# Two of three patterns of VectorE's exponentials added by DMA in a two-branch attention kernel

## The chip, the cores and the metric

The kernel runs on one core of one Trainium2 chip. The metric is the device time of one execution in microseconds (us), the median of several runs; lower is better.

## What is computed

Two independent attention blocks on inputs of 2048 rows and 512 columns, 32 heads of 16 columns each; the two results stand side by side in the output. Branch A is linear attention, branch B is softmax attention:

```
# A
phi = lambda t: jnp.where(t > 0, t + 1, jnp.exp(t)) + 1e-6
kv = jnp.einsum("bhsd,bhse->bhde", pk, v)
num = jnp.einsum("bhqd,bhde->bhqe", pq, kv)
o = num / den
...
# B
scores = jnp.einsum("bhqd,bhkd->bhqk", q, k) * scale
p = _softmax(scores, axis=-1)
o = jnp.einsum("bhqk,bhkd->bhqd", p, v)
```

Each branch has its own projections (x times wqkv) ahead of this and an output projection (times wo) behind it. Most of the work is B: 32 heads times 2048 x 2048 scores, each through an exponential.

## The kernel before

**Tiling.** Branch B is cut into 32 units. A unit is four heads (one per group of 32 rows of TensorE) and 512 queries. It holds 64 blocks: four heads times sixteen tiles of 128 keys. A block is a 128 x 512 piece of transposed scores. For each block one score matmul (line 946) fills a bank of PSUM with 128 keys by 512 queries; an engine takes the exponential into SBUF; value matmuls (line 1355) multiply it with the values and add into one bank per unit. The values have 16 columns and a column of ones, which gives the sum of the exponentials. Matmuls of four heads run beside one another on TensorE, score matmuls in four row groups and value matmuls in four column groups.

**Two ways to an exponential.** ScalarE (line 1161) reads two or three adjacent banks and writes the exact exponential as 16-bit floats into the buffer PT of 25 blocks; each of its blocks needs one value matmul. VectorE (line 1065) scales and offsets a block's scores and writes them as 16-bit integers whose bits, read as 16-bit floats, approximate the exponential. To make the approximation better, three such patterns are summed: the base pattern, weighted by 1.55 (VW, held in a scaled copy VX of the values), and two patterns that are the same integers plus 328 and plus 656 (SHIFT). The additions are made by GpSimd (line 1245) on the integers, four at a time as one 64-bit word; two blocks form a group, and one addition makes one pattern of a group. So a VectorE block needs three value matmuls: one with VX for the base pattern, two with VV for the shifted patterns. The buffer DI holds eight groups of three patterns (planes) of 2 x 512 values each.

**Order.** All instructions of all engines are written out at build time by a planner. It keeps a clock for each engine (T), a cost for each operation, candidates for each engine, and picks step by step what starts next; what it picks is appended to that engine's list. Each engine runs its list in order, and semaphores are derived from what is read and written. The choices around the change:

- `d_pick` (line 1004) decides whether a block goes to VectorE: a bank must be free, VectorE's and GpSimd's backlogs must be under limits (DBL, PBL), and a DI buffer must be free.
- `fill_act_cand` (line 1094) fills score banks for ScalarE, and puts blocks for VectorE beside them.
- `chain` (line 1199) follows when a group is complete; its inner `on_pool` (line 1221) emits the two additions, and `plain` (line 1214) would make them on VectorE late in the last unit.
- `pv_cand` (line 1282) batches value matmuls whose inputs are planned to be ready, up to a few rounds of four.
- Jobs for the projections, branch A and the outputs are filled in between. Their transfers are issued by SyncE, and a job that depends on one becomes available after a planned time: 6.5 us for the spread of the keys (line 678), 7.0 us for a transposed piece of A's input (line 482), 2.6 us for a transpose of A's output (line 859).
- The table SEG (line 274) holds 28 settings of the planner for each 12 us of planned time: limits, priorities, round sizes, and a seed for small random choices.

The costs that the planner uses are constants, among them:

```
PFX = 0.173
PEL = 0.00041
...
d = 0.0635 + w * 0.000833
...
waiting[bi] = (buf, b, push("dve", en + LTO["pe", "dve"], 0, 0.598, p1))
```

An addition is planned at PFX plus PEL for each of its 16-bit elements, an exponential on ScalarE at d for w columns, one on VectorE at 0.598 us, a round of value matmuls at 0.2185 us.

Of the kernel before, what the change touches and what calls it, by code (L numbers as in the profile page):

```python
# [10 lines left out]
F16 = mybir.dt.float16  # L11
# [228 lines left out]
def bass_concat_heads__linear_attn_block__softmax_full_mha__prompt_kernel(nc, A_x, A_wqkv, A_wo, B_x, B_wqkv, B_wo, out):  # L240
# [8 lines left out]
    LAY = (25, 8)  # L249
    PW = 0.5  # L250
# [6 lines left out]
    NDG = LAY[1]  # L257
# [9 lines left out]
    DE3 = 0  # L267
# [87 lines left out]
    XAL = 7.0  # L355
# [10 lines left out]
    TRACE = None  # L366
    PEB = 14
# [7 lines left out]
    with es:  # L375
# [19 lines left out]
        DIR = 3 * DGW  # L395
        DI = sb("DI", [128, NDG * DIR], I16)

        def di_at(v, b):

            return b * DIR + v * DGW  # L400
# [166 lines left out]
        port = {"pool": 0.0, "dve": (0.0, 0.0)}  # L567

# [84 lines left out]
        def proj_job(Gp, sc, kind, fast=False, **kw):  # L653
# [24 lines left out]
            def spread(bk):  # L678
                for e_ in range(2):
# [4 lines left out]
            st.append(("dma", 6.5, spread))  # L684
# [75 lines left out]
        def chunked(st, i):  # L760

            eng, dur, fn = st[3]
            def done(bk):
                fn(bk)
                xa_left[i] -= 1
                if xa_left[i] == 0 and i + 2 < 12:
                    load_xa(i + 2)
                    tok[("xA", i + 2)] = T["pe"] + XAL
            st[3] = (eng, dur, done)
            return st  # L770
# [27 lines left out]
        def akvsum_job(hp, bl, **kw):  # L798
# [7 lines left out]
            if hp == bl == 1:  # L806
                st.append(("dma", 14.0, lambda bk: load_wo()))
# [24 lines left out]
        def anum_job(sc, tl, **kw):  # L832
            pq = sc % 2
            o2 = tl % 2
            def f(e, bk):
                for bq in range(4):
# [6 lines left out]
                            RD[:, pq, tl * 32:tl * 32 + 32].unsqueeze(2).broadcast_to([128, 32, 16]), op=ALU.mult), [("RD", pq)], oak(o2))), ("dma", 2.6, lambda bk: ont_load(o2))],  # L843
# [15 lines left out]
        def ont_load(o2):  # L859
# [943 lines left out]
```

## Time and profile before

| what | value |
|---|---|
| median of 3 runs (range) | 644.63 us (644.21 to 644.69) |
| the profiled execution | 644.23 us |
| its span, first to last instruction | 642.5 us |
| mean granted TensorE clock | 0.998 |
| DMA packets, bytes | 53230, 21.80 MB |

The profile is one execution. Its page lists, for each engine, the time that it was busy and its share of the span; then groups of instructions by line of the kernel, with the count, the busy time, the mean duration of one in ns, and the idle time of that engine just before them with what ended it. A duration includes a tail in which the next instruction already runs, so the time that an instruction costs is read from the distance between starts in the timeline. In the stretches, each engine has its busy time and its count in parentheses; the last three columns are the granted clock, the mean busy share of the 16 DMA engines, and GB/s.

### The profile page before, as it was taken

How to read it: one execution, taken by the hardware profiler on the slowest of the kernel's cores; microseconds unless marked ns; L12 is line 12 of the kernel's file. 1: busy time of each engine (PE TensorE's matmuls, PEld its weight loads, DVE VectorE, ACT ScalarE, POOL GpSimd, SP SyncE). 2: the span in 40 equal slices, each digit the busy share in tenths (PEclk: the TensorE clock that was granted, in tenths of full speed). 3: DMA queues.
4: the chain of work that ended last, by engine and by line, in shares of the span. 5: the costliest groups of instructions: out<-in, count | busy, mean ns of one | idle time of the engine just before them, and what ended most of it. 6: DMA issues, size and time to landing. Idle time of an engine off the chain costs nothing.

```text
span 642.5 us, 20026 instructions
## 1 busy us (share of the span) xinstructions
PE 635.4 (99%) x8562; PEld 218.1 (34%) x8562; DVE 612.0 (95%) x1086; ACT 628.7 (98%) x692; POOL 440.5 (69%) x751
## 2 busy tenths in 40 slices
PE   8999999999999999999999999999999999999997
PEld 6333332333333333343333333223222322223243
DVE  6999999999999999999999999999999999999985
ACT  6999999999999999999999999999999999999995
POOL 4666788876767766657767676677776668766751
PEclk9999999999999999999999999999999999999999
DMA  9701000002010011012021012002110110000112
GB/s 187 209 2 24 21 1 12 8 3 43 3 35 1 2 35 35 10 35 45 18 50 51 3 41 45 17 10 50 28 34 10 27 34 18 26 11 26 35 43 71
DMA packets 53230, 21.80 MB, mean 34 GB/s; under 512 B 44176, under 2 KB 52624, under 8 KB 53136
## 3 DMA queue, kind: packets, MB, share of 16 engines
q1 hardware_dynamic: 51664, 19.80, 13.3%
q8 instruction: 69, 1.13, 0.7%
q10 hardware_dynamic: 1472, 0.66, 0.4%
q14 instruction: 25, 0.20, 0.1%
HBM read 4.46 MB, written 4.19 MB: 13 GB/s over the span
## 4 chain that ended last, share of the span: by engine, by line
PE 68%; ACT 31%; DVE 1%; issue 0%
ACT PT L1161 30%; PE pS L946 22%; PE pD L1355 20%; PE pD L636 7%; PE pPV L1355 4%; PE pS L636 4%; PE pPV L636 3%; PE pD L735 1%; PE pS L943 1%; ACT EA L751 1%; PE pD L946 1%; PE pD L1479 1%; PE pS L735 1%; PE pPV L946 0%; PE pD L1348 0%; PE pPV L1348 0%
## 5 line engine op out<-in xcount | busy, mean ns | idle before, releaser
L1161 ACT ACTIVATE PT<-pS 128x1024 f16<-128x1024 f32 (+1 forms) x655 | 615.4, 1082 | 1.3 <-PE pS L946 1.0
L1245 POOL INT64_ADD DI<-DI x726 | 433.2, 610 | 187.5 <-DVE DI L1065 184.2
L946 PE MATMUL pS<-QT,KM 32*128 32x512 bf16 x1512 | 255.1, 384 | 1.4 <-ACT PT L1161 0.5
L1065 DVE TENSOR_SCALAR DI<-pD 128x512 int16<-128x512 f32 (+1 forms) x288 | 193.5, 681 | 6.9 <-PE pD L946 2.1
L1355 PE MATMUL pD<-PT,VV 128*17 128x512 f16 x979 | 178.0, 381 | 0.0
L1355 PE MATMUL pD<-DI,VV 128*17 128x512 f16 x1114 | 176.8, 381 | 0.0
L1065 DVE TENSOR_SCALAR DI<-pS 128x512 int16<-128x512 f32 x235 | 159.1, 677 | 2.1 <-PE pS L946 1.3
L946 PEld LDWEIGHTS pS<-QT,KM 32*128 32x128 bf16 x1512 | 65.2, 91 | 231.3 <-ACT PT L1161 191.9
L1065 DVE TENSOR_SCALAR DI<-pPV 128x512 int16<-128x512 f32 x199 | 135.0, 678 | 4.6 <-PE pPV L946 2.5
L1355 PE MATMUL pD<-DI,VX 128*17 128x512 f16 x557 | 129.2, 382 | 0.0
L946 PE MATMUL pD<-QT,KM 32*128 32x512 bf16 x275 | 102.8, 384 | 0.0
L946 PE MATMUL pPV<-QT,KM 32*128 32x512 bf16 x197 | 75.7, 384 | 0.0
L1355 PE MATMUL pPV<-PT,VV 128*17 128x512 f16 x299 | 52.0, 381 | 0.0
L1355 PEld LDWEIGHTS pD<-DI,VV 128*17 128x17 bf16 x1114 | 38.9, 88 | 33.6 <-issue 22.3
L1355 PEld LDWEIGHTS pD<-PT,VV 128*17 128x17 bf16 x979 | 39.0, 88 | 30.5 <-issue 24.9
L1355 PE MATMUL pPV<-DI,VV 128*17 128x512 f16 x298 | 49.3, 381 | 0.0
L1355 PEld LDWEIGHTS pD<-DI,VX 128*17 128x17 bf16 x557 | 28.5, 88 | 17.9 <-issue 14.4
L1355 PE MATMUL pPV<-DI,VX 128*17 128x512 f16 x149 | 34.2, 382 | 0.0
L946 PEld LDWEIGHTS pD<-QT,KM 32*128 32x128 bf16 x275 | 24.3, 90 | 1.9 <-DVE DI L1065 0.7
L946 PEld LDWEIGHTS pPV<-QT,KM 32*128 32x128 bf16 x197 | 17.8, 90 | 1.9 <-DVE DI L1065 1.4
L636 PE MATMUL pD<-Wa,xTa 128*32 128x256 bf16 x448 | 18.1, 275 | 0.0
L636 PE MATMUL pS<-Wa,xTa 128*32 128x256 bf16 x448 | 18.0, 275 | 0.0
(202 smaller groups left out, 534.1 us busy)
## 6 DMA issues: line engine op xcount, KB each, us to landing
out_dram<-KNa SPq DMA_DIRECT2D x31, 128.0 KB, 1.8
Wa<-in_A_wqkv_dram SPq DMA_DIRECT2D x1, 1536.0 KB, 8.7
KM<-KR SPq DMA_DIRECT2D x96, 16.0 KB, 1.8
Wb<-in_B_wqkv_dram SPq DMA_DIRECT2D x2, 384.0 KB, 5.6
Wb<-in_B_wqkv_dram SPq DMA_DIRECT2D x1, 512.0 KB, 4.6
Wa<-in_A_wo_dram SPq DMA_DIRECT2D x1, 512.0 KB, 4.4
Wa<-in_B_wo_dram SPq DMA_DIRECT2D x1, 512.0 KB, 3.7
ON<-in_B_x_dram ACTq DMA_DIRECT2D x1, 256.0 KB, 2.8
```

The costliest lines, as they stand in the source:

```text
L636: ins = self.e.matmul(out_[32 * g:32 * g + 32], lhsT=lhsT[:, 32 * g:32 * g + 32], rhs=rhs, start=start, stop=stop, tile_position=(0, 32 * g))
L735: return e.matmul(f32v(bk)[:, tl * 128:(tl + 1) * 128], lhsT=xTb[:, cc, t * 128:(t + 1) * 128], rhs=Wb[:, cc, 1024 + Gp * 128:1024 + Gp * ...
L751: ("act", 0.0635 + n * 0.000833, f_ev("act", lambda e, bk: e.activation(EA[:, 0:n], f32v(bk)[:, c0:c0 + n], ACTF.Exp), [], ["EA"])),
L943: ins = e.matmul(dst[:, 256 * i:256 * i + 256], lhsT=KM[32 * g:32 * g + 32, Gp % 2, e_, (2 * jp + i) * 128:(2 * jp + i + 1) * 128], rhs=QT ...
L946: return e.matmul(dst, lhsT=KM[32 * g:32 * g + 32, Gp % 2, e_, j * 128:(j + 1) * 128], rhs=QT[32 * g:32 * g + 32, Gp % 2, c * 512:(c + 1) ...
L1065: sch.add("dve", lambda e, db_=DBANK[b0]: e.tensor_scalar(DI[:, di_at(0, buf) + i * 512:di_at(0, buf) + (i + n) * 512], f32v(db_, n * 512) ...
L1161: sch.add("act", lambda e: e.activation(PTf[:, p0 * 512:p0 * 512 + w], S5[:, c0:c0 + w], ACTF.Exp, scale=SC), reads=skeys(sl, len(bl)), wr ...
L1245: sch.add("pool", lambda e, v=v, word=word: e.int64_add(at64(v), at64(0), word), reads=keys, writes=[("DI", v, x) for x in best])
L1355: sch.add("pe", lambda e, g=g, j=j, c0=c0, V_=V_, r2=r2, P=P, first=first, last_=last_, pb_=pvb[0]: e.matmul(pb_[0][32 * g:32 * g + 17, pb ...
L1479: ins = e.matmul(f32v(wb_, 128), lhsT=ZW[:], rhs=ZW[:], start=True, stop=True)
```

## The change

For groups that are "joined", the two shifted patterns are made by GpSimd as before, and then GpSimd issues a DMA that adds the third pattern's plane onto the second's in 16-bit floats. Value matmuls then read the base pattern and the sum: two for each block in place of three. A group is joined if planned time is past 36 us (DMB), GpSimd's backlog is under 6 us (PDM), and it is not the last unit with under 30 blocks left (DMT). The issue is planned 0.66 us (SWT2) after the additions end, as a candidate of GpSimd of its own, so that the next group's additions, if they are ready, come ahead of it.

The planes of DI are no longer tied together by group: there are 9 base, 9 first shifted and 6 second shifted planes, each held and freed by its own users, and additions wait in the plan until planes are free (`plane_gate`). Two groups can share additions and the DMA where both are ready (`best` has at most two members now). The planner keeps a clock for the DMA engines (`dma_free`), to which a sum adds 0.00137 us per column and the other transfers 0.6 to 4.0 us, and plans a sum's landing behind it. Jobs wait longer for their transfers in the plan: 8.0, 10.0 and 4.5 us in place of 6.5, 7.0 and 2.6. The path `plain` is gone. SEG has new values in nearly all rows, with start times that are no longer multiples of 12, and so the whole order of the program is another. The last row starts at 624.352 (before: 624.0).

The diff, cut to its core:

```diff
-    LAY = (25, 8)
-    PW = 0.5
+    LAY = (25, (9, 9, 6))
+    PW = 0.8
...
+    PDM = 6.0
+    DMT = 30
+    PDF = 0.58
+    PDG = 0.4
+    SWT2 = 0.66
+    DMB = 36.0
+    SDB = 0.00137
+    SDM = 1.5
+    NSL = 6
...
-        DIR = 3 * DGW
-        DI = sb("DI", [128, NDG * DIR], I16)
+        DI = sb("DI", [128, sum(NPL) * DGW], I16)
...
+        dma_free = [0.0]
+
+        def dma_busy(t, d):
+
+            dma_free[0] = max(dma_free[0], t) + d
...
+        def plane_pick(v, n, t):
+
+            fr = sorted((x, b) for b, x in enumerate(pfree[v]) if x is not None)[:n]
+            return sorted(b for x, b in fr) if len(fr) == n and fr[-1][0] <= t else None
...
+                joined = st_ >= DMB and p_backlog(st_) < PDM and not (u_min(items) == NU - 1 and left[NU - 1] < DMT)
+                for v in (1, 2):
+                    for x in slots[v]:
+                        plane_hold(v, x, 1 if joined and v == 2 else n)
                     word = int.from_bytes(struct.pack("<4H", *[SHIFT[v - 1]] * 4), "little")
-                    sch.add("pool", lambda e, v=v, word=word: e.int64_add(at64(v), at64(0), word), reads=keys, writes=[("DI", v, x) for x in best])
+                    sch.add("pool", lambda e, v=v, word=word: e.int64_add(at64(v), at64(0), word), reads=keys, writes=[("DI", v, x) for x in slots[v]])
                     T["pool"] = st_ = st_ + PFX + len(best) * w * PEL
...
+                if joined:
+                    for it in items:
+                        for b in it:
+                            pv_due[b[0]][b[2]] -= 1
...
+                    def add(st_, en_):
+                        lane = sum_lanes[nsum[0] % len(sum_lanes)]
+                        nsum[0] += 1
+                        sch.add(lane, lambda e: e.dma_start(at16(1), at16(2), accum_op=ALU.add), reads=[("DI", 2, x) for x in slots[2]], writes=[("DI", 1, x) for x in slots[1]], queue="pool")
+                        dma_free[0] = max(st_ + 0.9, dma_free[0]) + len(best) * w * SDB
+                        land = dma_free[0] + 1.0 + SDM
+                        for x, it in zip(slots[1], items):
+                            give(x, it, 1, land)
+                        for x in slots[2]:
+                            plane_done(2, x, land)
+                    push("pool", st_ + SWT2, -1, PDF + (PDG if len(best) > 1 and any(sl[1] - sl[0] > 1 for sl in slots[1:]) else 0.0), add)
```

Six semaphore lanes (NSL) serve the sums in turn; a sum on a lane also waits for the one before it on that lane.

More of the change, by code (lines that the diff above doesn't have):

```diff
@@ L256, in bass_concat_heads__linear_attn_block__softmax_full_mha__prompt_kernel @@
     DG = 2
-    NDG = LAY[1]
+    NPL = LAY[1]
     VW = 1.5546875
@@ L354, in bass_concat_heads__linear_attn_block__softmax_full_mha__prompt_kernel @@
     SLK = {}
-    XAL = 7.0
+    XAL = 10.0
     NZ = 0
@@ L394, in bass_concat_heads__linear_attn_block__softmax_full_mha__prompt_kernel @@
         DGW = DG * 512
-        DIR = 3 * DGW
-        DI = sb("DI", [128, NDG * DIR], I16)
+        DI = sb("DI", [128, sum(NPL) * DGW], I16)
         def di_at(v, b):
-            return b * DIR + v * DGW
+            return (sum(NPL[:v]) + b) * DGW
         DW = DI.bitcast(mybir.dt.uint64)
@@ L678, in spread @@
             def spread(bk):
+                dma_busy(T["dve"], 0.6)
                 for e_ in range(2):
@@ L683, in spread @@
                                 reads=[("KR", kr)], writes=[("KM", r, e_, sc, g)] + ([("KMj", e_, j, g) for j in range(4)] if r == sc == 0 else []), queue="sp")
-            st.append(("dma", 6.5, spread))
+            st.append(("dma", 8.0, spread))
             return Job(st, needs, [(5, ("K", Gp, 0, sc)), (5, ("K", Gp, 1, sc)), (5, ("krd", ki))], rel=4, **kw)
@@ L767, in done @@
                     load_xa(i + 2)
+                    dma_busy(T["pe"] + 2.0, 3.0)
                     tok[("xA", i + 2)] = T["pe"] + XAL
@@ L806, in akvsum_job @@
             if hp == bl == 1:
-                st.append(("dma", 14.0, lambda bk: load_wo()))
+                st.append(("dma", 14.0, lambda bk: (dma_busy(T["dve"] + 1.0, 4.0), load_wo())))
             return Job(st, [(k_, hp, t) for k_ in ("ak", "av") for t in range(0, NT, 2)], [(3, ("akv", hp, bl)), (5, ("rha", bq))] + ([(6, "WO")] if hp == bl == 1 else []), rel=5, **kw)
@@ L842, in anum_job @@
                             OA[:, o2, :].rearrange("p (h e) -> p h e", e=16), f32v(bk).rearrange("p (h e) -> p h e", e=16),
-                            RD[:, pq, tl * 32:tl * 32 + 32].unsqueeze(2).broadcast_to([128, 32, 16]), op=ALU.mult), [("RD", pq)], oak(o2))), ("dma", 2.6, lambda bk: ont_load(o2))],
+                            RD[:, pq, tl * 32:tl * 32 + 32].unsqueeze(2).broadcast_to([128, 32, 16]), op=ALU.mult), [("RD", pq)], oak(o2))), ("dma", 4.5, lambda bk: ont_load(o2))],
                        [("aden", sc)] + ([("aout", 4 * sc + tl - 2)] if 4 * sc + tl >= 2 else []),
@@ L859, in ont_load @@
         def ont_load(o2):
+            dma_busy(T["dve"] + 1.0, 0.6)
             sch.add(ont_lane, lambda e: e.dma_start_transpose(ONT[:, o2, :].rearrange("p (c n) -> p c n", n=128), OA[:, o2, :]),
@@ L978, in bass_concat_heads__linear_attn_block__softmax_full_mha__prompt_kernel, with plane_hold, plane_done, plane_gate @@
         dgroup = {"n": 0, "buf": 0, "open": False}
-        dgfree = [0.0] * NDG
-        dgleft = [0] * NDG
+        pfree = [[0.0] * n for n in NPL]
+        dgfree = pfree[0]
+        pusers = [[0] * n for n in NPL]
+        plast = [[0.0] * n for n in NPL]
+        def plane_hold(v, b, n):
+            pfree[v][b] = None
+            pusers[v][b] += n
+        def plane_done(v, b, t):
+            pusers[v][b] -= 1
+            plast[v][b] = max(plast[v][b], t)
+            if pusers[v][b] == 0:
+                pfree[v][b] = plast[v][b]
+                plast[v][b] = 0.0
+        def plane_pick(v, n, t):
+            fr = sorted((x, b) for b, x in enumerate(pfree[v]) if x is not None)[:n]
+            return sorted(b for x, b in fr) if len(fr) == n and fr[-1][0] <= t else None
+        def plane_gate():
+            g = [min((x for x in pfree[v] if x is not None), default=None) for v in (1, 2)]
+            return None if None in g else max(g)
         def cur_unit():
@@ L1016, in d_pick @@
             if not dgroup["open"]:
-                buf = min((i for i in range(NDG) if dgfree[i] is not None), key=lambda i: (dgfree[i] > at, (i - dgroup["buf"] - 1) % NDG), default=None)
+                buf = min((i for i in range(NPL[0]) if dgfree[i] is not None), key=lambda i: (dgfree[i] > at, (i - dgroup["buf"] - 1) % NPL[0]), default=None)
                 if buf is None or dgfree[buf] > at:
@@ L1033, in d_take @@
                 dgroup["n"] += 1
-                dgfree[buf] = None
-                dgleft[buf] = 0
+                plane_hold(0, buf, 1)
                 dgroup["st"][buf] = {"taken": 0, "closed": False, "items": []}
@@ L1038, in d_take @@
             s_["taken"] += 1
-            dgleft[buf] += 3
+            plane_hold(0, buf, 1)
             if s_["taken"] == DG:
@@ L1072, in p1 @@
                         dfree[x] = en_ + LPE["dve"]
-                        pv_ready[b_[0]].append((en_ + LPE["dve"], b_, (DI.bitcast(F16)[:, di_at(0, buf) + k_ * 512:di_at(0, buf) + (k_ + 1) * 512], ("DI", 0, buf, k_)), ("d", buf), "X"))
+                        pv_ready[b_[0]].append((en_ + LPE["dve"], b_, (DI.bitcast(F16)[:, di_at(0, buf) + k_ * 512:di_at(0, buf) + (k_ + 1) * 512], ("DI", 0, buf, k_)), ("d", 0, buf), "X"))
                     s_["t"] = en_
@@ L1079, in bass_concat_heads__linear_attn_block__softmax_full_mha__prompt_kernel @@
         pshift = []
+        nsum = [0]
+        sum_lanes = [sch.new_dma_lane() for _ in range(NSL)]
+        DF = DI.bitcast(F16)
         pv_give = {}
@@ L1203, in chain, with give @@
             s_["chained"] = True
-            late = left[NU - 1] < DE3 and all(b[0] == NU - 1 for b in s_["items"])
             n = len(s_["items"])
             w = 512 * n
-            rk = [("DI", 0, buf, i) for i in range(n)]
-            def give(buf_, v, lane, en_):
-                for i, b in enumerate(dgroup["st"][buf_]["items"]):
-                    P = DI.bitcast(F16)[:, di_at(v, buf_) + i * 512:di_at(v, buf_) + (i + 1) * 512]
-                    pv_ready[b[0]].append((en_ + (LPE["pool"] if lane == "pool" else LPE["dve"]), b, (P, ("DI", v, buf_)), ("d", buf_), "V"))
-            def plain(v):
-                def run(st_, en_):
-                    sch.add("dve", lambda e: e.tensor_scalar(DI[:, di_at(v, buf):di_at(v, buf) + w], DI[:, di_at(0, buf):di_at(0, buf) + w], 1.0, float(SHIFT[v - 1]), op0=ALU.mult, op1=ALU.add),
-                            reads=rk, writes=[("DI", v, buf)])
-                    give(buf, v, "plain", en_)
-                return run
+            def give(slot, items, v, t):
+                for i, b in enumerate(items):
+                    P = DI.bitcast(F16)[:, di_at(v, slot) + i * 512:di_at(v, slot) + (i + 1) * 512]
+                    pv_ready[b[0]].append((t, b, (P, ("DI", v, slot)), ("d", v, slot), "V"))
             def on_pool(st_, en_):
-                near_ = {x[1]: x for x in pshift if x[2] == w and x[3][0] <= st_ + PMW}
+                near_ = {x[0]: x for x in pshift if x[1] == w and x[2][0] <= st_ + PMW}
                 near_[buf] = me[0]
                 best = [buf]
-                for step in range(1, NDG):
-                    run_ = [buf]
-                    while len(run_) < JN and run_[-1] + step in near_:
-                        run_.append(run_[-1] + step)
-                    while len(run_) < JN and run_[0] - step in near_:
-                        run_.insert(0, run_[0] - step)
-                    if len(run_) > len(best):
-                        best = run_
-                keys = []
+                for b2 in sorted(near_, key=lambda b2: near_[b2][2][0]):
+                    if b2 != buf and len(best) < JN and plane_pick(1, 2, st_) and plane_pick(2, 2, st_):
+                        best = sorted((buf, b2))
+                keys, items = [], []
                 for b_ in best:
@@ L1237, in on_pool @@
                     if b_ != buf:
-                        cands["pool"].remove(x[3])
-                        st_ = max(st_, x[3][0])
+                        cands["pool"].remove(x[2])
+                        st_ = max(st_, x[2][0])
                     keys += [("DI", 0, b_, i) for i in range(n)]
-                at64 = lambda v: bass.AP(DW, DW[:, di_at(v, best[0]) // 4:].offset, [list(DW[:, 0:1].ap[0])] +
-                                         ([[(best[1] - best[0]) * DIR // 4, len(best)]] if len(best) > 1 else []) + [[1, w // 4]])
@@ L1243, in on_pool, with at64, at16 @@
-                for v in vs:
+                    items.append(dgroup["st"][b_]["items"])
+                slots = [best] + [plane_pick(v, len(best), st_) for v in (1, 2)]
+                def at64(v):
+                    sl = slots[v]
+                    return bass.AP(DW, DW[:, di_at(v, sl[0]) // 4:].offset, [list(DW[:, 0:1].ap[0])] +
+                                   ([[(sl[1] - sl[0]) * DGW // 4, 2]] if len(sl) > 1 else []) + [[1, w // 4]])
+                def at16(v):
+                    sl = slots[v]
+                    return bass.AP(DF, DF[:, di_at(v, sl[0]):].offset, [list(DF[:, 0:1].ap[0])] + ([[(sl[1] - sl[0]) * DGW, 2]] if len(sl) > 1 else []) + [[1, w]])
@@ L1246, in on_pool @@
                     T["pool"] = st_ = st_ + PFX + len(best) * w * PEL
-                    for x in best:
-                        pv_give[x, v](st_)
-            vs = (1, 2)
-            if late:
-                for v in vs:
-                    push("dve", s_["t"], -2, 0.06 + w * 0.00027, plain(v))
-                return
-            for v in vs:
-                pv_give[buf, v] = lambda en_, v=v: give(buf, v, "pool", en_)
-            me = [(vs, buf, w, push("pool", s_["t"] + LTO["dve", "pool"], 0, len(vs) * (PFX + w * PEL), on_pool), rk)]
+                    if not joined:
+                        for x, it in zip(slots[v], items):
+                            give(x, it, v, st_ + LPE["pool"])
@@ new lines, in on_pool @@
+                for x in best:
+                    plane_done(0, x, st_ + LPE["pool"])
+                if joined:
+                    for it in items:
+                        for b in it:
+                            pv_due[b[0]][b[2]] -= 1
+                            if b[0] == LU:
+                                half_due[b[1] // 8][b[2]] -= 1
+                    def add(st_, en_):
[9 more added lines that the diff above has]
+                    push("pool", st_ + SWT2, -1, PDF + (PDG if len(best) > 1 and any(sl[1] - sl[0] > 1 for sl in slots[1:]) else 0.0), add)
@@ L1257, in chain, with u_min @@
+            def u_min(items):
+                return min(b[0] for it in items for b in it)
+            me = [(buf, w, push("pool", s_["t"] + LTO["dve", "pool"], 0, 2 * (PFX + w * PEL), on_pool))]
             pshift.append(me[0])
@@ L1362, in run @@
                     if src[0] == "d":
-                        dgleft[src[1]] -= 1
-                        if dgleft[src[1]] == 0 and dgroup["st"][src[1]]["closed"]:
-                            dgfree[src[1]] = en
+                        plane_done(src[1], src[2], en)
                     else:
@@ L1639, in bass_concat_heads__linear_attn_block__softmax_full_mha__prompt_kernel @@
             opts = []
+            gate = plane_gate()
             for eng in T:
@@ L1642, in bass_concat_heads__linear_attn_block__softmax_full_mha__prompt_kernel @@
                 for c_ in cands[eng]:
-                    st = max(pe_at("v" if isinstance(c_[3], Rounds) else "j") if eng == "pe" else T[eng], c_[0])
+                    if eng == "pool" and c_[1] == 0 and gate is None:
+                        continue
+                    st = max(pe_at("v" if isinstance(c_[3], Rounds) else "j") if eng == "pe" else T[eng], c_[0], gate if eng == "pool" and c_[1] == 0 else 0.0)
                     k_ = (round(st / 0.05), c_[1], c_[2])
```

106 rows, old and new, of the table SEG are left out of this document.

## The prediction

> **What bounds the kernel now.** I read the page of the profile first, then the stretches of time, the waits, the timeline of a steady part, and the DMA part.
>
> ```profile
> span 642.5 us, 20026 instructions
> ...
> PE 635.4 (99%) x8562; PEld 218.1 (34%) x8562; DVE 612.0 (95%) x1086; ACT 628.7 (98%) x692; POOL 440.5 (69%) x751
> ...
> PE 68%; ACT 31%; DVE 1%; issue 0%
> ...
> L1161 ACT ACTIVATE PT<-pS 128x1024 f16<-128x1024 f32 (+1 forms) x655 | 615.4, 1082 | 1.3 <-PE pS L946 1.0
> L1245 POOL INT64_ADD DI<-DI x726 | 433.2, 610 | 187.5 <-DVE DI L1065 184.2
> ...
> L1065 DVE TENSOR_SCALAR DI<-pD 128x512 int16<-128x512 f32 (+1 forms) x288 | 193.5, 681 | 6.9 <-PE pD L946 2.1
> ...
> L1355 PE MATMUL pD<-DI,VV 128*17 128x512 f16 x1114 | 176.8, 381 | 0.0
> L1065 DVE TENSOR_SCALAR DI<-pS 128x512 int16<-128x512 f32 x235 | 159.1, 677 | 2.1 <-PE pS L946 1.3
> ...
> L1065 DVE TENSOR_SCALAR DI<-pPV 128x512 int16<-128x512 f32 x199 | 135.0, 678 | 4.6 <-PE pPV L946 2.5
> ...
> L1355 PE MATMUL pD<-DI,VX 128*17 128x512 f16 x557 | 129.2, 382 | 0.0
> ```
>
> Three engines are nearly full at once: TensorE (PE) 99%, ScalarE (ACT) 98%, VectorE (DVE) 95%. Only GpSimd (POOL) has room, and it spends it waiting for VectorE (184.2 us). The chain that ended last alternates between PE and ACT. The stretches say where the little idle time lies:
>
> ```profile
> 8.00:40.00 32.00, 31.15 (x397) 12.25 (x397) 29.52 (x53) 31.49 (x33) 18.35 (x35) 1.00 0.67 156
> 40.00:600.00 560.00, 559.41 (x7484) 184.39 (x7483) 545.39 (x956) 559.68 (x621) 397.75 (x667) 1.00 0.10 24
> ...
> 625.00:643.00 18.00, 13.15 (x229) 6.53 (x224) 9.58 (x20) 10.06 (x11) 3.66 (x7) 0.93 0.22 64
> ```
>
> From 40 to 600 us ACT is idle for 0.3 us, VectorE for 14.6 us. So no relief of PE by itself ends the kernel earlier: ACT must be given less to do, and the only engine that can take blocks of exponentials from it is VectorE. The waits say how close PE runs to ACT:
>
> ```profile
> PEld pS L946 <- ACT PT L1161: 191.9, 481, 0.6
> POOL DI L1245 <- DVE DI L1065: 184.2, 220, 5.3
> ```
>
> 481 times the score matmuls waited on average 0.40 us for ACT to free a score buffer: that is PE's cushion before each fill.
>
> **The prices.** The steady part gives the pitch of each operation (the duration in the page includes a tail that overlaps the next one):
>
> ```profile
> 301.50 0.69 DVE L1065 TENSOR_SCALAR DI<-pD 128x512 int16<-128x512 f32 x1
> 302.10 0.68 DVE L1065 TENSOR_SCALAR DI<-pS 128x512 int16<-128x512 f32 x1
> ```
> ```profile
> 299.76 12.86 ACT PT L1161 x14
> ```
> ```profile
> 299.52 1.20 POOL L1245 INT64_ADD DI<-DI  x2 [0.59 <-DVE DI L1065]
> ```
> ```profile
> 300.49 0.38 PE L1355 MATMUL pD<-PT,VV 128*17 128x512 f16 x1
> ...
> 300.71 0.38 PE L1355 MATMUL pD<-DI,VV 128*17 128x512 f16 x1
> ```
>
> VectorE: 0.60 us a block. ACT: 12.86/14 = 0.919 us for two blocks, 0.459 a block. GpSimd: 0.60 us an addition. PE: 0.22 us from one round of up to four value matmuls to the next, 0.055 each. The planner's constants for these are 0.598, 0.9165, 0.593 (0.173 + 1024 x 0.00041) and 0.2185: within 1.2% of the rows. That is why I use its constants where the trace has no row.
>
> **Removed.** One value matmul per VectorE block whose group is summed. Sums are allowed from planned time 36 us until the last unit has under 30 blocks left, about the stretch 40 to 600:
>
> ```profile
> 40.00:600.00 560.00, 419.65 (x664) 1.00 0.10 24
> ```
>
> This is line 1065 alone: 664 blocks, 332 groups. 664 x 0.055 = 36.5 us of PE if all are summed and the rounds stay full; half of that if half are. It is a gain of capacity, not of time, since ACT is full beside it. The shortcut by which VectorE did late additions itself (line 1216) goes too; 726 additions for 363 groups stand on GpSimd now, so it was not used and costs nothing.
>
> **Added on GpSimd.** One DMA issue per group or per pair of groups. No row of before shows one there. The nearest are SyncE's own issues:
>
> ```profile
> 627.79 0.34 SPq L871 DMA_DIRECT2D out_dram<-KNa  x1
> 628.98 1.96 SPq L860 DMA_TRANSPOSE KNa<-VNa  x1
> ```
>
> Bounds 0.34 us (a plain 128-row transfer, the nearest in shape) to 1.96 us. I take the planner's 0.58, on the side of the plain transfer. 332 x 0.58 = 193 us, with 433.2 us of additions 626 of 642 us: full, but pairs save 0.173 us on each of two additions, and the planner sums only while GpSimd's backlog is under 6 us. The issue sits behind the next group's additions, so those do not wait for it; the third group's can wait 0.6 us, and behind them only value matmuls that have other work ahead.
>
> **Added on the DMA engines.** A group's plane is 128 x 1024 x 2 B = 256 KB. Rows for its price:
>
> ```profile
> out_dram<-KNa SPq DMA_DIRECT2D x31, 128.0 KB, 1.8
> ...
> ON<-in_B_x_dram ACTq DMA_DIRECT2D x1, 256.0 KB, 2.8
> ```
>
> In the stretch 8 to 40 the DMA engines moved 156 GB/s at a share of 0.67, so 233 GB/s when full: 1.13 us for 256 KB, or 2.25 us if reading both operands of the addition counts twice. The planner's 0.00137 x 1024 = 1.40 us lies between, nearer the lower; I take it. 332 x 1.40 = 465 us; with the 0.10 of 560 that is there now, 521 of 560 us. Tight, and worst beside the input and weight transfers. From issue to use the planner allows 0.9 + 1.40 + 1.0 + 1.5 = 4.8 us, against 2.8 us for the 256 KB load. The Trainium skill, "DMA: Bandwidth & Descriptors", section "Anatomy of one DMA", gives 2.0 us plus bytes over 436e3 per us for a DMA issued from GpSimd, by estimate 2.6 us here; the 2.8 us row agrees in size, no row shows an accumulating one, and by it a lone sum lands with 2 us to spare, so the forecast below stands.
>
> **Moved.** The 24 planes of the same total size are now 9 base, 9 first-pattern, 6 second-pattern, freed separately. 332 groups in 560 us is one per 1.7 us; a second-pattern plane is held for two additions, 0.66 us, 0.58 us and 4.8 us, 7.2 us, so 4.3 of 6 on average: it covers. Longer planned waits for the key spread, the A-side loads and transposes (6.5 to 8, 7 to 10, 2.6 to 4.5 us) only shift when their jobs become available; other jobs cover them. If that cover failed, 16 transposes x 1.9 = 30 us of waiting would be spread over PE; the A jobs are a reserve for gaps, so I put 0, end 0 to +2 us.
>
> **The sum.** With PE relieved, VectorE can be fed whenever it is free. Moving x blocks saves 0.459x on ACT and adds 0.60x on VectorE, while the span shrinks too: using all 14.6 us gives x = 14.6/1.059 = 13.8 and 6.3 us; leaving 1% of the stretch (5.6 us) idle gives x = 8.5 and 3.9 us. I take 11 blocks: 11 x 0.459 = 5.0 us. Start and end give 0: sums are off there, and in the last stretch the work is a string of single steps. The profiled execution took 644.23 us (span 642.5), the median is 644.63, so the same 5.0 us off the median: 639.6.
>
> **Rivals.**
> *Late sums (slower).* PE takes its queue in order. A value matmul whose sum has not landed stops the score matmuls behind it; after the cushion of 0.40 us ACT runs dry, and its time is never made up, as it has only 0.3 us idle in 560. A sum that queues behind one other group's transfer beyond the plan is 1.40 us late and costs 1.0 us. One in 25 of 332 is 13 us: 639.6 + 13 = 653. It decides from 5 in all, 1 in 66. For it: GpSimd and the DMA engines both planned above 90%, an issue price without a row. Against: 1.5 us of margin in the plan and prices elsewhere within 1.2%.
>
> *No block moves.* PE gets idle time, VectorE's idle time turns out to be waits for projections and transposes, ACT keeps its 655 instructions: 644.6. The same comes out if the change hardly does what it says because GpSimd's backlog mostly forbids sums. For it: ACT is the full engine already. Against: VectorE waits for PE's matmuls in its rows.
>
> *GpSimd or DMA overrun (much slower).* At 1.2 us an issue, 332 x 0.62 = 206 us more than planned: 626 + 206 = 832 us of GpSimd, about 835. At 2.25 us a group the DMA engines need 747 + 56 = 803 us for 560, about 885. One way to the first: issuing waits for VectorE's instruction. Rows against: additions take 0.60 us beside back-to-back VectorE evictions from PSUM; only SBUF-to-SBUF rows are left,
>
> ```profile
> L752 DVE TENSOR_SCALAR EC<-EA 128x528 bf16<-128x528 bf16 x32 | 13.5, 423 | 0.8
> ...
> L742 DVE TENSOR_SCALAR VX<-VV 128x561 bf16<-128x561 bf16 x16 | 6.9, 439 | 0.1
> ```
>
> 20.4 us, 3% of the span: some 11 of 332 issues held for at most 0.44 us, under 5 us of GpSimd time. The rule is the Trainium skill's, "SBUF — State Buffer", section "Who interferes with whom": a VectorE instruction in a two-port mode holds the port pair that GpSimd also needs, and descriptor writing waits. The additions' 0.60 us show no such hold by the evictions; none here shows it for an issue.
>
> *More than forecast.* VectorE filled entirely, and idle tails of 0.08 us (0.68 against 0.60) recovered at each gap: 8 to 10 us, 635. It belongs to the forecast's side.
>
> **How the numbers follow.** Forecast (faster, 633.5 to 642): 0.68. No block moves: 0.11. Late sums: 0.17. Overrun: 0.04. A measurement of this kernel can tell about 0.2%, 1.3 us, from no change. Faster 0.68, same 0.11, slower 0.21. Range: down to 633.5 for the full use of VectorE, up to 653 for the late sums at the price above; beyond it the overrun and worse lateness, some 0.1, and below it 0.05. The forecast's own range is 634 to 642.
>
> **What would show it.** Right: in the bank pD, value matmuls reading DI with VV (the shifted patterns) now stand to those with VX (the base pattern) as 1114 to 557, two to one; after, nearer one to one. Exponentials on ACT down by about 5 instructions of two blocks; VectorE above 98% from 40 to 600; ACT still at 99.9%; PE below 97%; GpSimd, issues counted, above 90%.
>
> Wrong: waits of value-matmul weight loads for a DMA in the waits, and ACT idle behind them (late sums); ACT's count unchanged (no move); GpSimd issue rows above 1 us or a DMA share near 1 (overrun).

## The result and the profile after

| | before | after |
|---|---|---|
| median (range), 4 runs each | 644.46 us (644.21 to 644.69) | 716.26 us (715.7 to 717.59) |
| ratio, 95% interval | | 1.112 [1.110, 1.113] |
| span of the profiled execution | 642.5 us | 714.1 us |
| granted TensorE clock, mean | 0.998 | 0.951 |

The change made the kernel 71.8 us slower; 639.6 was predicted, with 653.0 as the upper end.

The page of after: span, busy times, DMA shares in 40 slices, the queue of GpSimd's DMAs, the chain by engine, and groups of instructions.

```profile
span 714.1 us, 18885 instructions
...
PE 650.4 (91%) x7894; PEld 217.4 (30%) x7894; DVE 619.8 (87%) x1085; ACT 638.3 (89%) x686; POOL 666.4 (93%) x873
...
DMA  9559798998889798997999998989898899999571
...
q0 software_dynamic: 45216, 87.31, 72.6%
...
POOL 64%; PE 17%; DMA 7%; DVE 5%; ACT 3%; issue 1%; ACTq 0%; POOLq 0%
...
L1204 ACT ACTIVATE PT<-pS 128x1024 f16<-128x1024 f32 (+1 forms) x649 | 624.6, 1072 | 58.9 <-PE pD L962 23.3
L1286 POOL INT64_ADD DI<-DI x582 | 567.2, 1759 | 27.3 <-DVE DI L1105 25.3
L1303 POOL DMA_DIRECT2D DI<-DI x266 | 425.5, 1896 | 1.9 <-POOL DI L1286 1.4
...
L1413 PE MATMUL pD<-DI,VV 128*17 128x512 f16 x470 | 84.4, 395 | 31.3 <-DMA DI<-DI 30.9
L1413 PE MATMUL pD<-DI,VX 128*17 128x512 f16 x453 | 95.7, 394 | 0.1
```

The chain tells it first: before, PE and ACT held 99% of it and GpSimd (POOL) nothing; now GpSimd holds 64%. It waited 187.5 us ahead of its additions before and 27.3 us now. The other engines all have room: ACT fell from 98% to 89%, with 58.9 us of idle time ahead of its exponentials in place of 1.3. The change did what it says: value matmuls with VV now stand to those with VX nearly one to one (470 to 453) in this bank, where it was two to one.

The durations of GpSimd's two groups can't be added up: 567.2 + 425.5 is 993 us of a 714 us span, because a record there begins while the instructions ahead of it still run. What an instruction costs is read in the chain, where only one thing stands at a time (start, duration, what, how many):

```profile
101.14 1.73 POOL DI L1303 x2
...
116.50 1.24 POOL DI L1286 x2
117.74 0.83 POOL DI L1303
118.58 1.24 POOL DI L1286 x2
119.82 0.83 POOL DI L1303
...
169.75 3.26 POOL DI L1286 x4
...
177.98 2.10 POOL DI L1303 x2
```

Two additions take 1.24 us, 0.62 each (0.60 before), and an issue 0.83 us where 0.58 was planned. A group costs GpSimd 2.07 us. The piece of four holds two paired additions: 3.26 - 1.24 = 2.02, 1.01 each. Two issues in a row take 1.73 us where both are of one group (0.83, and 0.90 for the second), and 2.10 us where the first is of a pair. By the shapes in the trace and the distance from the end of the instruction ahead, 54 pairs whose planes lie apart take 1.17 us each in median, and 13 pairs in neighbouring planes the same 0.83 as one group.

The waits of after, and its stretch from 40 to 690 us (columns PE, PEld, DVE, ACT, POOL, granted clock, DMA share, GB/s):

```profile
PEld pD L1413 <- DMA DI<-DI: 46.2, 46, 2.2
...
PE pD L1413 <- DMA DI<-DI: 30.9, 32, 1.8
...
POOL DI L1286 <- DVE DI L1105: 25.3, 19, 5.5
ACT PT L1204 <- PE pD L962: 23.3, 27, 3.3
...
PEld pPV L1413 <- DMA DI<-DI: 11.8, 16, 2.3
...
PE pPV L1413 <- DMA DI<-DI: 7.0, 9, 2.0
```
```profile
40.00:690.00 650.00, 597.79 (x7155) 190.48 (x7153) 576.28 (x994) 593.66 (x640) 636.75 (x815) 0.95 0.90 157
```

GpSimd is busy for 98% of that stretch. Its sums come late, the value matmuls wait for them in PE's queue, and ACT and VectorE run dry behind PE. (The waits of PEld and of PE overlap: the weight loads wait 58 us for sums, and in 38 us of these PE itself is idle.) The waits for "DMA" name the last step of that chain of causes, not the first.

### The profile page after: what moved, and what is told of

It reads as the page before. It is cut to its first block, busy times and chain, and to the rows that moved or that the text cites. A ratio compares the mean times of both kernels' runs of the same rounds, so it can differ in the third digit from the quotient of the medians.

```text
span 714.1 us, 18885 instructions
## 1 busy us (share of the span) xinstructions
PE 650.4 (91%) x7894; PEld 217.4 (30%) x7894; DVE 619.8 (87%) x1085; ACT 638.3 (89%) x686; POOL 666.4 (93%) x873
## 3 DMA queue, kind: packets, MB, share of 16 engines
q0 software_dynamic: 45216, 87.31, 72.6%
## 4 chain that ended last, share of the span: by engine, by line
POOL 64%; PE 17%; DMA 7%; DVE 5%; ACT 3%; issue 1%; ACTq 0%; POOLq 0%
POOL DI L1286 40%; POOL DI L1303 25%; PE pS L962 5%; DMA DI<-DI 5%; ACT PT L1204 3%; PE pD L1413 3%; DVE DI L1105 3%; PE pPV L1413 2%; DMA KNa<-VNa 1%; PE pD L649 1%; PE pS L649 1%; PE pPV L649 1%; PE pD L749 1%; DMA Wb<-in_B_wqkv_dram 1%; PE pPV L1406 1%
## 5 line engine op out<-in xcount | busy, mean ns | idle before, releaser
L1204 ACT ACTIVATE PT<-pS 128x1024 f16<-128x1024 f32 (+1 forms) x649 | 624.6, 1072 | 58.9 <-PE pD L962 23.3
L1286 POOL INT64_ADD DI<-DI x582 | 567.2, 1759 | 27.3 <-DVE DI L1105 25.3
L1303 POOL DMA_DIRECT2D DI<-DI x266 | 425.5, 1896 | 1.9 <-POOL DI L1286 1.4
L1105 DVE TENSOR_SCALAR DI<-pD 128x512 int16<-128x512 f32 x336 | 225.2, 682 | 32.9 <-PE pD L962 20.3
L962 PE MATMUL pD<-QT,KM 32*128 32x512 bf16 x323 | 123.5, 397 | 1.9 <-DVE DI L1105 1.4
L1413 PE MATMUL pD<-PT,VV 128*17 128x512 f16 x827 | 122.3, 395 | 0.0
L1105 DVE TENSOR_SCALAR DI<-pPV 128x512 int16<-128x512 f32 x159 | 108.5, 683 | 15.4 <-PE pPV L962 9.7
L1413 PE MATMUL pD<-DI,VV 128*17 128x512 f16 x470 | 84.4, 395 | 31.3 <-DMA DI<-DI 30.9
L1413 PE MATMUL pD<-DI,VX 128*17 128x512 f16 x453 | 95.7, 394 | 0.1
L1413 PEld LDWEIGHTS pD<-DI,VV 128*17 128x17 bf16 x470 | 18.9, 89 | 62.8 <-DMA DI<-DI 46.2
L649 PE MATMUL pD<-xTb,Wb 128*32 128x512 bf16 x304 | 23.6, 384 | 0.1
```

The lines of the kernel that those rows point to most:

```text
L649: ins = self.e.matmul(out_[32 * g:32 * g + 32], lhsT=lhsT[:, 32 * g:32 * g + 32], rhs=rhs, start=start, stop=stop, tile_position=(0, 32 * g))
L962: return e.matmul(dst, lhsT=KM[32 * g:32 * g + 32, Gp % 2, e_, j * 128:(j + 1) * 128], rhs=QT[32 * g:32 * g + 32, Gp % 2, c * 512:(c + 1) ...
L1105: sch.add("dve", lambda e, db_=DBANK[b0]: e.tensor_scalar(DI[:, di_at(0, buf) + i * 512:di_at(0, buf) + (i + n) * 512], f32v(db_, n * 512) ...
L1204: sch.add("act", lambda e: e.activation(PTf[:, p0 * 512:p0 * 512 + w], S5[:, c0:c0 + w], ACTF.Exp, scale=SC), reads=skeys(sl, len(bl)), wr ...
L1286: sch.add("pool", lambda e, v=v, word=word: e.int64_add(at64(v), at64(0), word), reads=keys, writes=[("DI", v, x) for x in slots[v]])
L1303: sch.add(lane, lambda e: e.dma_start(at16(1), at16(2), accum_op=ALU.add), reads=[("DI", 2, x) for x in slots[2]], writes=[("DI", 1, x) fo ...
```

## The experiments

The theories: **G**, GpSimd is over full because an issue costs it more than planned; **D**, the DMA engines are over full or slow, and the sums land late for that reason; **C**, fewer value matmuls leave PE thinly filled, and the granted clock falls. The expectations below also name **O**, the new order as such is slow; **C2**, the clock falls at a few thin places of that order; and **F**, the order is longer for other reasons than the clock. All but e1, e9 and e12 leave a part of the computation out; it is named with each.

**The sums off.** Nothing left out; all groups take the way with three value matmuls.

```diff
-    PDM = 6.0
+    PDM = -1.0
```

> No group is joined (the backlog limit PDM is set below zero): the new planes, planner and settings stay, GpSimd issues no DMA, value matmuls are three per VectorE block again. Theory G (GpSimd overruns: an issue holds it 0.83 us, not 0.58, and it has no room for that) and theory D (the DMA engines are too full: 256 KB takes about 1.56 us of them, not 1.40): both expect 642 to 660 us, since the settings were not chosen for this. Theory O (the new order itself is the cause): above 690.

656.52 us, ratio 1.019 [1.016, 1.022]. The new layout of planes and the new settings, which belong to an order with sums, lose 12 us without one DMA. VectorE takes fewer blocks (1055 instructions in place of 1086). So the slowdown of 71.8 comes with the sums, but a comparison with this run doesn't give their price, as the order is another one. The next runs therefore keep the order of after.

**Small sums.** Each sum moves 16 columns of a plane (128 rows of 32 B); the rest of the third pattern is left out.

```diff
-...at16(v)... [[1, w]])
+...at16(v)... [[1, 16]])
```

> Same order of every engine; each sum moves only 16 columns of a plane, 128 rows of 32 bytes, in place of 1024 (the rest of the third pattern is left out of the result). The issue stays, the transfer all but goes. Theory G: 690 to 716 us, GpSimd still 90% busy. Theory D: 637 to 655. Theory O: 700 or more.

716.12 us, ratio 1.111 [1.102, 1.121]: with almost no bytes, no gain at all. Its stretch 40 to 600, and its chain:

```profile
40.00:600.00 560.00, 517.14 (x6301) 168.96 (x6298) 499.69 (x867) 513.34 (x560) 554.03 (x710) 0.96 0.23 25
```
```profile
105.41 1.24 POOL DI L1286 x2
106.66 0.83 POOL DI L1303
107.49 1.24 POOL DI L1286 x2
108.73 0.83 POOL DI L1303
```

The DMA share is 0.23 in place of 0.90, GpSimd 99% busy, and the issue costs the same 0.83 us for 4 KB as for 256 KB. D falls.

**Short additions.** Full sums; but once a plane has been written in full, additions write an eighth of its columns, so most of the shifted patterns are old values.

```diff
+                aw = w if full else w // 8
...
-... + [[1, w // 4]])
+... + [[1, aw // 4]])
```

> Same order of every engine and the same full sums; after each plane was written once in full, GpSimd's additions write only an eighth of the columns (the rest of the patterns are left from earlier groups). An addition falls from 0.62 to about 0.23 us, 582 of them give GpSimd some 230 us of room. Theory G: 637 to 660 us. Theory D: 690 or more, DMA share still 0.9. Theory O: 700 or more.

658.54 us, ratio 1.022 [1.018, 1.026]. The stretch:

```profile
40.00:600.00 560.00, 546.53 (x6818) 180.74 (x6815) 538.95 (x945) 554.75 (x611) 356.73 (x776) 0.98 1.00 174
```

All 333 units of 256 KB are moved, the DMA engines are 100% busy, and no value matmul waits for a sum any more. 57.7 us of the 71.8 are GpSimd's. O, which expects 700 or more, falls too: the order is that of after.

**Both of these together**, to see what the order gives with neither cost.

> Short additions and small sums together, the same order of every engine: neither GpSimd nor the DMA engines can limit. This is what the order itself would give if its prices held. My forecast of 639.6 expects 634 to 643 us here; theory O expects 690 or more. Between 643 and 648 would say that the order had nothing to gain even undisturbed.

655.58 us, ratio 1.017 [1.014, 1.020]: the expected 634 to 643 was missed. Even with GpSimd at 61% and the DMA engines nearly free, this order is 11 us behind the kernel before. The later runs look for these 11 us.

**Every second sum not issued**, same order; the third pattern of those groups is left out.

```diff
+                        if nsum[0] % 2 == 0:
                           sch.add(lane, lambda e: e.dma_start(at16(1), at16(2), ...
```

> The changed kernel with the same order, but every second sum is not issued (its third pattern is left out of the result). GpSimd is relieved of about 133 issues, 118 us of 651. Theory G: 655 to 672 us, waits for sums nearly gone. Theory D was already at odds with the small sums; it would expect about 680 to 700 here, as half of the DMA load remains.

653.6 us, ratio 1.014 [1.012, 1.016], better than expected. With 133 issues GpSimd is busy for 533.2 us (82%), and the loss is gone but for the same 9 to 11 us. Halving the one suspected cost, with additions whole, gives what shortening the additions gave: it is GpSimd's total that counts.

**Value matmuls left out of the kernel before**: its own order, without the matmul of the second shifted pattern wherever it is neither first nor last of an accumulation. It gives PE the relief of the change and nothing else; the third pattern is left out.

```diff
-                    else:
+                    elif first or last_ or pk[:2] != ("DI", 2):
                       sch.add("pe", ...
```

> The kernel before in its own order, with the value matmul of the second shifted pattern left out (that pattern is missing in the result), some 680 of 2118: the relief of TensorE alone, no sums, no DMA, nothing moved. My forecast's term (a gain of capacity, not of time): 643.3 to 645.9 us, no difference. Theory C: granted clock below 0.99 and 647 to 660 us, slower by doing less.

643.6 us, ratio 0.998 [0.997, 0.999]. Some 700 matmuls fewer (7866 in place of 8562) are worth 0.8 us:

```profile
PE 632.1 (98%) x7866; PEld 216.2 (34%) x7866; DVE 611.6 (95%) x1086; ACT 627.7 (98%) x692; POOL 440.6 (69%) x751
```

And the granted clock stays at 1.0, so fewer matmuls alone don't lower it: C in its plain form falls.

**The planner told the measured price.** Nothing left out; the order is another one.

```diff
-    PDF = 0.58
-    PDG = 0.4
-    PDM = 6.0
+    PDF = 0.84
+    PDG = 0.21
+    PDM = 2.0
```

> The changed kernel planned with an issue at 0.84 us (1.05 for a separate pair) and sums only while GpSimd's backlog is under 2 us in place of 6; the settings table, chosen for other prices, stays. Theory G: waits for sums under 15 us in all and 650 to 668 us, near the 656.5 of no sums with this table. If the price were not the cause: above 690.

660.62 us, ratio 1.025 [1.023, 1.027]. The plan now has 123 sums, GpSimd is 80% busy, PE waits 0.2 us for sums in all; yet it loses 16 us, 4 more than with no sum. The seeds and limits of SEG belong to another plan, so this is no verdict on the best order at this price. It does show the issue where GpSimd has room, so that its record holds little waiting:

```profile
L1303 POOL DMA_DIRECT2D DI<-DI x123 | 109.1, 887 | 20.2 <-POOL DI L1286 18.7
```

**Where the 9 to 11 us went.** In the same stretches of 8 us (from 288, 336, 472, 512 and 624 on) e5 and e7 show a mean clock of 0.58 to 0.79 and ACT short of work; by the trace's clock records the clock is at half for 3.4 us in the first three and for 6.8 us in the other two. Two of them in e7, then the first of these two in the kernel before:

```profile
336.00:344.00 8.00, 7.76 (x80) 2.14 (x78) 6.68 (x14) 6.74 (x9) 5.77 (x8) 0.79 0.32 56
...
512.00:520.00 8.00, 7.83 (x66) 1.69 (x62) 6.93 (x13) 6.58 (x7) 5.97 (x8) 0.60 0.58 100
```
```profile
336.00:344.00 8.00, 8.00 (x105) 2.76 (x106) 7.61 (x15) 8.00 (x10) 6.24 (x11) 1.00 0.45 133
```

From 336 on PE has 80 matmuls in place of 105; a part of that is the slower clock itself. e6 adds matmuls with zero weights behind the batches of e5 (first diff); e10 and e11 let the planner fill shorter planned gaps of PE with dummy matmuls in e5 and e7 (second diff).

```diff
+                for g, P, pk in extra:
+                    sch.add("pe", lambda e, g=g, P=P, pb_=pvb[0]: e.matmul(..., lhsT=ZW[:, 0:17], rhs=P[:, 0:256], start=False, stop=False, ...), ...)
```
```diff
-    FIDLE = 0.8
+    FIDLE = 0.2
```

> The run with short additions and small sums (655.6 us, clock 0.977) with, behind each batch of value matmuls, one more matmul of 256 columns with zero weights for each sum in it: it adds nothing to the result but keeps TensorE working. Theory C (with a third of VectorE's value matmuls gone TensorE has gaps, its granted clock drops to half for some us at a time, and this is what holds the undisturbed order above 644): clock 0.99 or more, 642 to 650 us. Theory F (the order is simply longer): 654 to 665, since work is only added.

> The run with short additions and small sums (655.6 us), same order of all work; the planner only drops dummy matmuls of zeros (256 columns, 206 in all) into planned gaps of TensorE from 0.2 us on, where before it did so from 0.8 us on and there were none. Theory C2 (the new order leaves TensorE thin at a few fixed places, there its granted clock halves for about 3.4 us, and that makes most of the 11 us by which the undisturbed order is behind the kernel before): fewer than three dips, clock 0.99 or more, 644 to 650 us. Theory F (the order is longer for other reasons): 653 to 660, whatever the clock.

> The run with every second sum left out (653.6 us, dips at the same places as with small sums) with the same dummy matmuls in planned gaps from 0.2 us on. Theory C2: 643 to 649 us and clock 0.99 or more. Theory F: 651 to 658.

e6: 666.46 us, 1.035 [1.033, 1.036], a miss: 539 added matmuls cost more time than the clock gave back (0.985 against 0.977), so it tells nothing of C. e10: 651.81 us, 1.012 [1.010, 1.014]; e11: 650.47 us, 1.010 [1.009, 1.012]. Both have a clock of 0.995 or more and dips nearly gone, and gain 3.8 and 3.1 us, between what C2 and F expected: the dips at thin places of this order are real, but a third of the 9 to 11 us.

**The end of the program.** The issue of the last store is the last work that all of these kernels start. Before, 3.4 us of span follow it (642.5 - 639.13), with the sums 8.65 us; the store itself lands 2.4 and 3.7 us after its issue:

```profile
639.13 0.33 SPq L1471 DMA_DIRECT2D out_dram<-KNa  x1
```
```profile
705.45 0.33 SPq L1527 DMA_DIRECT2D out_dram<-KNa  x1
```

e12 puts small DMAs of GpSimd into the order of before, nothing left out:

```diff
+                if st_ >= 36.0 and len(stores) < 28:
+                    small[0] += 1
+                    if small[0] % 2:
+                        i = small[0] // 2 % 4
+                        sch.add(small_lanes[i], lambda e, i=i: e.dma_start(IC.bitcast(BF)[0:16, 16 * i:16 * i + 16], ZW[0:16, 0:16]), ..., queue="pool", ...)
```

> The kernel before, with a small DMA (16 rows of 32 B, between two buffers that nothing else uses then) issued by GpSimd behind every second group's additions from planned 36 us on, 176 in all; the plan does not know of them, so the order is that of before. Nothing is left out of the computation. Two questions. (1) The end: in the runs with 266 DMAs from GpSimd the span went on 7.2 to 8.7 us after the start of the last store, with 123 or 133 of them 5.3 to 6.0, with none 3.2 to 3.7: about 17 ns for each. If the number of DMAs does it, 176 give 3.4 + 3.0 = 6.4 us, and the time is 644.5 + 3 = 647.5, more only if value matmuls wait for additions. If the changed order's end does it, the tail stays at 3.4 us. (2) The price of an issue: if it is a fixed 0.83 to 0.87 us, GpSimd has 440 + 176 x 0.85 = 590 us of work in 642 and still fits; if it goes by rows (16 here, 128 in the sums), an issue takes 0.1 to 0.3 us and GpSimd stays under 500 us.

651.95 us, ratio 1.011 [1.010, 1.013].

```profile
L1255 POOL DMA_DIRECT2D IC<-ZW x176 | 88.3, 501 | 2.0 <-issue 2.0
```
```profile
40.00:600.00 560.00, 557.71 (x7447) 184.20 (x7439) 543.63 (x950) 557.21 (x617) 468.17 (x830) 1.00 0.11 24
```
```profile
642.51 0.39 SPq L1478 DMA_DIRECT2D out_dram<-KNa  x1
```

These are the group of the added DMAs on the page, the stretch from 40 to 600 and the last store in the timeline. The span ends at 650.2, 7.7 us behind the last store: the longer end comes with GpSimd's DMAs, not with the changed order. It costs 4.3 us of the 7.45 here. But "17 ns for each" falls: 176 small DMAs give 7.7 us, 266 of the sums 7.2 to 8.7, and e13, below, 5.3 with 266. What sets its length stays open. The rest, 3.1 us, is probably GpSimd again: it is 80% busy, the weight loads of value matmuls wait 11.8 us for its additions in place of 7.1, and ACT loses 2.5 us from 40 to 600 (557.21 busy in place of 559.68).

**Sums of 16 rows** in the changed kernel; the third pattern's other rows are left out.

```diff
-... [list(DF[:, 0:1].ap[0])] ...
+... [[DF[:, 0:1].ap[0][0], 16]] ...
```

> The changed kernel with each sum over 16 of the 128 rows, same order; the rest of the third pattern is left out of the sum. An eighth of the rows, at the full 2 KB each. If the price of an issue goes by rows, it falls to 0.1 to 0.3 us, GpSimd has about 500 us of work, and the time comes near the 653.6 of every second sum: 648 to 660. If the price is fixed for each DMA, GpSimd stays over 90% busy and the time stays at 710 to 717, as it did when the bytes alone were cut.

671.72 us, ratio 1.042 [1.040, 1.044]: between the two expectations. The chain:

```profile
103.35 0.73 POOL DI L1303
104.08 1.24 POOL DI L1286 x2
105.32 0.73 POOL DI L1303
...
123.11 1.52 POOL DI L1303 x2
```

An eighth of the rows saves 0.10 us of 0.83, so most of the price of a single issue is fixed for each DMA. A pair with its planes apart falls further, from 1.17 to 0.78 us. Two issues in a row mostly take 1.52 or 1.61 us in place of 1.73 or 2.10. GpSimd's busy time fell from 666.4 to 623.8 us, by 42.6, and the time by 44.5: as long as GpSimd is the bound, its saving is the kernel's.

| run | GpSimd busy, us | time, us |
|---|---|---|
| after | 666.4 | 716.26 |
| small sums (e3) | 671.7 | 716.12 |
| sums of 16 rows (e13) | 623.8 | 671.72 |
| every second sum (e7) | 533.2 | 653.6 |
| short additions (e4) | 395.6 | 658.54 |

In the first three rows the time is GpSimd's busy time plus 44 to 50 us, and below them it no longer follows it. This is G, shown from both sides: less of either of GpSimd's two jobs takes the loss away, less for the DMA engines doesn't.

**The sum of the 71.8 us**: 58 to 60 are GpSimd's excess (after against e4, 57.7; against e7, 62.7 less the 2.7 by which e7's end is shorter), about 5 the longer end (8.65 - 3.4), 3 to 4 the clock at thin places as e5 and e7 show it, and 3 to 4 stay unexplained (e10 and e11 without their longer ends of 7.4 and 6.0 us, against 644.22 of the kernel before beside them: 651.81 - 644.22 - 4.0 = 3.6 and 650.47 - 644.22 - 2.6 = 3.6). The deeper fall of the clock in after (0.951, where e4 has 0.976) comes and goes with GpSimd's excess and is counted there. No run beat the kernel before with the whole computation; the relief itself is worth 0.8.

## Why the prediction was wrong

**The step that failed** is GpSimd's issue, "I take the planner's 0.58, on the side of the plain transfer", and with it "626 of 642 us: full". It measured 0.83 behind an addition, 0.93 behind another issue, and 1.17 for a pair whose planes lie apart. Added up in the trace, after's 442 single and 140 paired additions take 414 us of GpSimd and its 266 issues 245 us; with 7 us of other work that is the 666.4 of the page. By the plan's constants the same additions are 404 us and the issues 176 (0.58, and 0.98 for the pairs apart). The issues alone are 70 us dearer than planned, and 58 to 60 us were lost. The prediction had the mechanism as its rival "GpSimd or DMA overrun", at 0.04, with a price of 1.2 us; it needed far less. By the prediction's own sum the overrun begins at (642 - 433) / 332 = 0.63 us, 0.05 above the value taken, while the bounds of the price were 0.34 and 1.96. And that sum set the work against the whole span, though the 332 issues fall into the 560 us from 40 to 600. By the prediction's own row, additions fill 397.75 us of these, and 332 x 0.58 us of issues make 590 of 560: there the overrun begins at (560 - 397.75) / 332 = 0.49 us, below the value taken. Only the pairs made room: by the plan's constants after's 70 pairs save some 41 us of additions and issues.

**What the price is not.** The prediction named a cause for a dear issue, "issuing waits for VectorE's instruction". Of the 131 single issues that stand right behind an addition on a busy GpSimd, all but one take 0.80 to 0.86 us, counted from the end of that addition, whatever VectorE does meanwhile. So no hold by VectorE shows; what the 0.83 us consist of stays open. The sign "GpSimd issue rows above 1 us" would not have told of the overrun, as 0.83 was enough.

**Why 0.58 was believed.** "within 1.2% of the rows. That is why I use its constants where the trace has no row": good constants for four operations that ran before were no measure of a fifth that never had. The nearest rows were SyncE's issues, from another engine. The Trainium skill, "DMA: Bandwidth & Descriptors", section "Anatomy of one DMA", lists the generation of descriptors as "small, variable" in what a DMA takes from start to end. Here the issue holds GpSimd for 0.83 us, and for as much with 32 B rows as with 2 KB rows; the measurement decides. No run shows how much of it is that generation.

**The backlog limit.** "the planner sums only while GpSimd's backlog is under 6 us" was read as a protection. The backlog is counted on the plan's own clock, at the plan's price, so the real lateness never reached it.

**The 11 blocks, 5.0 us.** None moved. ScalarE has 6 exponentials fewer (649 in place of 655), which was named as a sign that it would be right. The groups by shape show more:

```profile
L1204 ACT ACTIVATE PT<-pS 128x1024 f16<-128x1024 f32 x620 | 588.2, 1053 | 54.8 <-PE pS L962 22.2 <-PE pD L962 21.9 <-PE pPV L962 8.6
L1204 ACT ACTIVATE PT<-pS 128x1536 f16<-128x1536 f32 x29 | 42.8, 1474 | 4.1 <-PE pS L959 1.7 <-PE pD L962 1.4 <-PE pS L962 1.0
```

620 of two banks and 29 of three are 1327 blocks, 2 more than before (640 and 15). The count of instructions was the wrong thing to look for. Even with GpSimd relieved, VectorE is 96% busy from 40 to 600 (539.2 us in e5, 539.8 in e7, of 560), not above 98%, and less than the 545.4 of before.

**Late sums** came as described, with 58 us of waits of weight loads and 38 us of idle time of PE inside them, but as a consequence: with GpSimd at 60% (e4) or 82% (e7) no wait of PE for a sum is left. The row "waits of value-matmul weight loads for a DMA" had been given as the sign of late sums alone; GpSimd's overrun shows the same sign, and only the chain and GpSimd's busy share tell them apart.

**The DMA engines' price** of 1.40 us was 1.56 (72.6% of 714.1 over 333 units). The page has sums landing 5.7 us (one group) and 6.1 us (pairs) behind the issue in median, but there the issue's record begins while the instruction ahead still runs. From the end of that instruction it is 4.4 and 5.3 us, where 4.8 and 6.2 (0.9 + 2.8 + 1.0 + 1.5) were planned on free DMA engines; in e7, with room on GpSimd, 3.4 and 5.1. 81 of after's 199 single sums did land later than 4.8 us, but the time to landing was not the error that decided. A "DMA share near 1" was named as a sign of overrun. e4 shows a share of 1.00 and no wait of PE for a sum, so that sign was wrong.

**Right** were "a gain of capacity, not of time" (e8: 696 matmuls, 0.8 us), and the ratio of value matmuls. "Start and end give 0" failed at the end by about 5 us.

## What to carry to other kernels

When a change fills an idle engine to over 95% in its own plan, work out the price at which it overflows before believing any price: here it lay 9% above the one assumed by the sum over the whole span, and below it by the sum over the stretch in which the operation runs, and the operation had no row in the trace. Set work against the time in which it can run, not against the span. Time a new operation on the engine that will issue it, once, with its real shape, before a planner builds on it. And relief for an engine that runs beside a full one is worth almost nothing until work has been shown to move.

## What the runs showed of the hardware

- A DMA issued by GpSimd behind an addition holds GpSimd for 0.83 us, at 128 rows, whether a row has 32 B or 2 KB (after, e3), and 1.17 us where each row has two pieces that lie apart; 0.73 and 0.78 us at 16 rows of 2 KB (e13); 0.44 us for 16 rows of 32 B without the addition, in another kernel (e12). These are distances between ends of instructions; e12's record of one lasts 0.50 us. What makes up the 0.29 between 0.73 and 0.44 was not separated.
- An accumulating transfer of 256 KB within SBUF took 1.56 us of all 16 engines' time. One of 4 KB landed 2.5 us behind the start of its issue's record in median with GpSimd at 61% (e5), and 3.5 with it full (e3), where the record holds more waiting.
- The program's end behind the last store was 3.2 to 3.7 us in the kernels without GpSimd DMAs, 5.3 to 8.7 in those with 123 to 266 of them, and not in proportion to the number. Of 3.4 and 8.65 us in before and after, 0.9 and 5.0 come behind the landing of the store.
- The clock fell to half for 3.4 us, a mean of 0.79 over 8 us, at a place where PE still was 97% busy by its records (whose ends are modelled) and had 80 matmuls in place of 105; the count sets no limit, as e7 had 71 at a clock of 1.00 from 464 to 472. The Trainium skill, "TensorE: Matmul & The Clock Gate", section "Part 1: The HAM clock gate", ties the lower clock to PE's activity in windows of about 3.4 us; these places, and their going with dummy matmuls (e10, e11), agree with that, but no run shows where the limit lies.
